# Pooled attention into a gated MLP on one core: transposing the probabilities on VectorE and by DMA instead of on TensorE

## The chip, the cores and the metric

The kernel runs on one core of a Trainium2 chip. The metric is the device time of one execution in microseconds (us); each version is timed in several executions, and the median counts. A profiled execution gives the trace from which all rows below are copied.

## The reference

Attention over pooled keys and values, 8 batches of 8 heads, 576 tokens, head size 64, and after it a multilayer product on all 4608 tokens:

```python
pool = 8                      # Sp = 576 / 8 = 72 pooled keys
k_p = k.reshape(B, H, Sp, pool, D).mean(axis=3)
v_p = v.reshape(B, H, Sp, pool, D).mean(axis=3)
scores = scale * np.matmul(q, k_p.transpose(0, 1, 3, 2))
attn = np.exp(scores - max); attn = attn / (sum + 1e-09)
x = np.matmul(attn, v_p)      # then (4608, 512), heads side by side
a = x @ w1;  b = x @ w2       # 512 -> 1024 each
out = ((a * b) @ w3) @ w_out  # 1024 -> 1024 -> 512
```

All arrays are float32. The kernel multiplies w3 and w_out once at the start, and it splits the operands of its products in a high and a low part of TensorE's 32-bit format (`F32R`), so that one product is three matmuls.

## The kernel before, in words

The 4608 tokens are cut into 12 chunks of 384. Three chunks hold two batches. Chunks 1, 4, 7, 10 contain the end of one batch and the start of the next, so their tokens go in four tiles of 96; the others go in three tiles of 128.

One plan orders everything. `at(kind, k, fn, ...)` puts a function at plan place `k`; the list is sorted by step (the whole part of `k`), within a step by kind (L loads, P work of the vector and scalar engines, M matmuls of the product, A matmuls of the attention), then by the fraction of `k`, then by the order of entry, and the functions are called in that order. Each engine executes its instructions in program order, and each DMA is issued by the SP queue in program order.

MoE chunk m takes 24 steps from M0 + 24 m: for each j of eight, `a_mm` (step 3j), `b_mm` (3j + 1) and `out_mm` of an earlier j (3j + 5), three steps of some 2.1 us on TensorE. Their results lie in PSUM tiles "a" and "b" of one buffer each: `a_post` (ScalarE, 3j + 1) copies a, `b_post` (3j + 2) multiplies it with b on VectorE (L545) and makes its high part on ScalarE (L546), `g_lo` (3j + 2.5) its low part on VectorE (L551). The bank of "b" is free for the next j when L545 is done. `out_post` of the chunk before stores its result at step 3.

Under MoE chunk m the attention of chunk n = m + 1 is prepared. For each tile t: `s_mm` computes the scores in two halves of four heads (TensorE, L404); `soft1` takes the minimum of a half, subtracts, exponentiates and sums (VectorE L420, L422, L426, ScalarE L425); `soft2` divides (L439, L441, L442), with the probabilities in E, a tile of 8 heads x 72 keys; `soft3` puts the 8 keys of each head that do not fit in the 64-key layout into R, high and low parts (L451, L453). Then `pt_mm` and `ptr_mm` transpose E (four 128-column blocks, L464) and R (two, L474) on TensorE into PSUM, and `pt_post` and `ptr_post` take them from there: ScalarE makes the high part PTh (L486) and copies the rest PTr (L491), VectorE subtracts for the low part PTl (L487). `av_mm` multiplies them with the pooled values for one pair of heads (L499 to L502), and `av_post` writes xT, the input of the next MoE chunk.

Beside that, in the same plan: queries are loaded by `load_q` (L265) and turned by VectorE block transposes in `tr_q` (L276); keys are loaded by `load_k` (L307) and summed over eight on GpSimd (`pool_tree`, L362 to L364); values by `load_v` and `load_vr` (L343, L356). For each batch `prep_v2` splits the pooled values on ScalarE (L374) and GpSimd (L375), and `prep_vr` sums the remaining values on GpSimd and then casts them on ScalarE (L381 to L384). For batches 2 to 7 they stand in steps 9, 10 and 10 of MoE chunks 2, 3, 5, 6, 8 and 9.

The places of a chunk's attention come from these lines at the end:

```python
s0, pt, av = (3, 5.5, 20.5) if n == 1 else (0, 6, 17) if nt == 4 else (0, 5, 15)
s_at = [k + s0 + 3 * t for t in range(nt)]
plan_att(n, s_at, 1, [x + pt for x in s_at], [k + av + pr for pr in range(NPR)])
```

In `p1`, every tile name has one buffer; in `p2`, two.

Of the kernel before, what the change touches and what calls it, by code (L numbers as in the profile page):

```python
# [8 lines left out]
F32 = mybir.dt.float32  # L9
F32R = mybir.dt.float32r  # L10
I32 = mybir.dt.int32
AF = mybir.ActivationFunctionType
ALU = mybir.AluOpType
# [5 lines left out]
def kernel(  # L19
# [14 lines left out]
    nc = tc.nc  # L34
# [3 lines left out]
    P = 128  # L38
# [3 lines left out]
    KR = KP - KM  # L42
    MK0 = (KR, 0)
    RK0 = (0, KM)
    NPR = H // 2
# [4 lines left out]
    CH = 384  # L50
# [9 lines left out]
    p1 = ctx.enter_context(tc.tile_pool(name="p1", bufs=1))  # L60
    p2 = ctx.enter_context(tc.tile_pool(name="p2", bufs=2))
# [9 lines left out]
    VR = [cp.tile([P, NPR, P], F32R, name=f"VR{i}") for i in range(2)]  # L71
# [4 lines left out]
        out=msk,  # L76
        in_=ident.rearrange("p (a two e) -> p two a e", two=2, e=2 * KR),
        axis=AX.XY,
        op=ALU.add,
# [8 lines left out]
    def f(ap):  # L88
        return ap.bitcast(F32)
# [11 lines left out]
    def W_cell(s, i, dt):  # L101
        return cp.tile([P, DM], dt, tag=f"W{s}_{i}", name="Wc")
# [48 lines left out]
    def split(src, hi, lo, eng=nc.vector):  # L151
        nc.scalar.copy(out=hi, in_=src)
        eng.tensor_tensor(out=lo, in0=src, in1=f(hi), op=ALU.subtract)  # L153

    def w_tiles(s):
        if s == 0:
            stage["wt"] = [t[:, i] for t, x in (
                (p1.tile([P, x, 512], I32, tag=tag, name="wt"), x)
                for tag, x in (("PTh", 3), ("PTl", 3), ("PTr", 1))) for i in range(x)]
        if s < NJ:  # L160
            stage["wo", s] = stage["wt"][s % 4], f(stage["wt"][4 + s % 3])
        stage["w3", s] = W_cell(0, 4 + s % 4, I32), W_cell(1, 4 + s % 4, F32)

    def w_block(v):
# [3 lines left out]
        if new:  # L168
            w_tiles(v)
            r3, z3 = stage["w3", v]  # L170
            ro, zo = stage["wo", v]
            high(raw["w3", v], z3)
            low(raw.pop(("w3", v)), r3)
            high(raw["wo", v], zo)
# [34 lines left out]
    def w_conv(s):  # L209
        w_tiles(s)  # L210
        conv_a(raw.pop(("w3", s)), *stage["w3", s])
# [28 lines left out]
    def pieces(n):  # L240
        i, r = divmod(n, 3)
        if r == 0:
            return [(2 * i, 0, 384, 0)]
        if r == 1:
            return [(2 * i, 384, 192, 0), (2 * i + 1, 0, 192, 192)]
        return [(2 * i + 1, 192, 384, 0)]

    def tok_tiles(n):
        res = []
        for (b, s0, cnt, off) in pieces(n):  # L250
            step = 128 if cnt == 384 else 96
            for x in range(0, cnt, step):
                res.append((b, off + x, step))
        return res
# [137 lines left out]
            nc.gpsimd.tensor_tensor(  # L392
                out=VR[b % 2][rows, r // 2::2, D * par:D * par + D], in0=hi[rows], in1=m[rows], op=ALU.add)

    Et, Mt, PTh, PTl, PTr, xT = {}, {}, {}, {}, {}, {}

    Sp = {}

# [35 lines left out]
    Rt = {}  # L434
# [10 lines left out]
    def soft3(n, t):  # L445
        b, off, nt = tok_tiles(n)[t]
        E = Et[n, t]
        R = Rt[n, t] = p2.tile([P, NPR, 2, 2, 2, KR], F32R, tag="R", name="R")
        er = E[:nt].rearrange("p (a h) (x e) -> p a (h x) e", h=2, e=KR)[:, :, 0:18:17, :]
        for dup in range(2):  # L450
            nc.scalar.copy(out=R[:nt, :, :, dup, 0], in_=er)  # L451
        for dup in range(2):
            nc.vector.tensor_tensor(  # L453
                out=R[:nt, :, :, dup, 1], in0=er, in1=f(R[:nt, :, :, dup, 0]), op=ALU.subtract)

    Tp = {}
# [11 lines left out]
    def ptr_mm(n, t):  # L468
        b, off, nt = tok_tiles(n)[t]
        R = f(Rt[n, t].rearrange("p a h u s e -> p (a h u s e)"))  # L470
        ps = patt.tile([P, 512], F32, tag="att", name="att")
        rv = ps[:, :2 * P].rearrange("p (a c) -> p a c", c=P)
        for g in range(2):
            nc.tensor.transpose(  # L474
                out=rv[:, g, :nt], in_=R[:nt, g * P:(g + 1) * P], identity=ident[:nt, :nt])
        Tp[n, t, "r"] = rv

    def pt_post(n, t):
        b, off, nt = tok_tiles(n)[t]
        if t == 0:  # L480
            PTh[n] = p1.tile([P, NPR, CH], F32R, tag="PTh", name="PTh")
            PTl[n] = p1.tile([P, NPR, CH], F32R, tag="PTl", name="PTl")
            PTr[n] = p1.tile([P, 2, CH], F32R, tag="PTr", name="PTr")
        pv = Tp.pop((n, t))
        hi, lo = PTh[n][:, :, off:off + nt], PTl[n][:, :, off:off + nt]
        nc.scalar.copy(out=hi, in_=pv[:, :, :nt])  # L486
        nc.vector.tensor_tensor(out=lo, in0=pv[:, :, :nt], in1=f(hi), op=ALU.subtract)  # L487

    def ptr_post(n, t):
        b, off, nt = tok_tiles(n)[t]  # L490
        nc.scalar.copy(out=PTr[n][:, :, off:off + nt], in_=Tp.pop((n, t, "r"))[:, :, :nt])  # L491

    def av_mm(n, pr):
        ps = patt.tile([P, 512], F32, tag="att", name="att")
        for (b, s0, cnt, off) in pieces(n):
            c = slice(off, off + cnt)
            vh, vl = (vbd[b % 2][s][:, pr] for s in range(2))
            o = ps[:, c]
            nc.tensor.matmul(out=o, lhsT=vh, rhs=PTh[n][:, pr, c], start=True, stop=False)  # L499
            nc.tensor.matmul(out=o, lhsT=vh, rhs=PTl[n][:, pr, c], start=False, stop=False)  # L500
            nc.tensor.matmul(out=o, lhsT=vl, rhs=PTh[n][:, pr, c], start=False, stop=False)  # L501
            nc.tensor.matmul(out=o, lhsT=VR[b % 2][:, pr], rhs=PTr[n][:, pr // 2, c], start=False, stop=True)  # L502
        Tp[n, pr, "x"] = ps

    def av_post(n, pr):
# [93 lines left out]
    def at(kind, k, fn, *args):  # L599


        plan.append((k // 1, "LPMA".index(kind), k % 1, len(plan), fn, args))

    def plan_att(n, s_at, ds, pt_at, av_at):


        for t in range(len(tok_tiles(n))):
            for half in range(2):
                k = s_at[t] + ds * half
                at("A", k, s_mm, n, t, half)  # L610
                at("P", k + 1, soft1, n, t, half)
            at("P", k + 2, soft2, n, t)
            at("P", k + 3, soft3, n, t)
            k = pt_at[t]
            at("A", k, pt_mm, n, t)
            at("A", k, ptr_mm, n, t)
            at("P", k + 1, pt_post, n, t)
            at("P", k + 1, ptr_post, n, t)
        for pr in range(NPR):
            at("A", av_at[pr], av_mm, n, pr)  # L620
            at("P", av_at[pr] + 1, av_post, n, pr)
# [17 lines left out]
    def plan_q(n, load, d_load, turn, d_turn):  # L639
        for pr in range(NPR):  # L640
            at("L", load + d_load * pr, load_q, n, (pr,))
            at("P", turn + d_turn * pr, tr_q, n, pr)

    def plan_q3(n, load, turn):
        for pr in range(NPR):
            at("L", load[pr], load_q3, n, pr)
            at("A", turn[pr], q3_turn, n, pr)
            at("P", turn[pr] // 1 + 1.2, q3_post, n, pr)
# [10 lines left out]
    for s in range(NS):  # L659
        k = F0 + 2 * s  # L660
# [3 lines left out]
        else:  # L664
# [9 lines left out]
    plan_q3(0, [K0 - 10.5 + 1.5 * pr for pr in range(NPR)], [K0 - 3, K0 - 2, K0 - 1, K0])  # L674
    plan_v(0, K0 - 4.5, K0 + 5.5, K0 + 2, K0 + 11, K0 + 8.5)
    plan_att(0, [K0 + 3, K0 + 2.5, K0 + 6.5], 0.5, [K0 + 6.5, K0 + 8.5, K0 + 11.5],
             [K0 + 14, K0 + 14.5, K0 + 14.5, K0 + 14.5])


    for j in range(NJ):  # L680
        for w in range(2):
            i = 2 * j + w
            at("L", K0 + 8.5 + i, load_w12, j, w)
            k = M0 - 6 + 1.25 * i
# [5 lines left out]
    for m in range(NCH):  # L690
        m0 = M0 + 3 * NJ * m
        for j in range(NJ):
            k = m0 + 3 * j
# [9 lines left out]
    for n in range(1, NCH):  # L703
        k = M0 + 3 * NJ * (n - 1)
        nt = len(tok_tiles(n))
        s0, pt, av = (3, 5.5, 20.5) if n == 1 else (0, 6, 17) if nt == 4 else (0, 5, 15)
        s_at = [k + s0 + 3 * t for t in range(nt)]
        plan_att(n, s_at, 1, [x + pt for x in s_at], [k + av + pr for pr in range(NPR)])
        if n == 1:
            plan_q3(n, [K0 + 8.5 + 1.5 * pr for pr in range(NPR)], [K0 + 12, K0 + 13, K0 + 15, K0 + 15.5])  # L710
        else:
            plan_q(n, k - 18, 1, k - 9, 1)
    for b in range(1, B):
        k = M0 + 3 * NJ * (3 * (b // 2) + b % 2 - 1)
# [39 lines left out]
```

## Time and profile before

| what | value |
|---|---|
| three executions, median | 807.12 us (804.91 to 807.75) |
| span of the profiled execution, first to last instruction | 803.4 us; its time with what lies around it is not listed apart, the lowest execution is 1.5 us above its span |
| mean granted TensorE clock | 0.989 |
| TensorE busy, matmuls | 777.9 us, 97% |
| VectorE busy | 431.7 us, 54% |
| ScalarE busy | 288.0 us, 36% |
| GpSimd busy | 196.1 us, 24% |
| DMA | 62.63 MB, 30.1% of 16 engines' span |

The page gives the busy share of each engine, the span in 40 slices, the chain of work that ended last, and the costliest groups of instructions. A row of a timeline has the start and the duration in us, the engine, the line and the operation, out<-in with partitions x elements, and in brackets how long the engine sat idle before it and which instruction ended that. A row of the chain has start, duration, engine, tile and line. A row of windows has the stretch, its length, busy time and count of TensorE's matmuls, its weight loads, VectorE, ScalarE and GpSimd, then the granted clock, the DMA share and GB/s. A row of groups has the count, then busy us, the mean ns of one, and the idle time before them. Durations of neighbours on one engine overlap a little; from start to next start is what an instruction takes from its queue.

### The profile page before, as it was taken

To read this page: it belongs to the slowest core of one execution; us is meant where nothing else is said; L and a number is where in the kernel's file an instruction comes from. 1 tells how busy PE (TensorE), PEld (TensorE's weight loads), DVE (VectorE), ACT (ScalarE), POOL (GpSimd) and SP (SyncE) were. 2 spreads that over 40 slices of the span, in tenths; PEclk is the share of its full clock that TensorE was granted. 3 is DMA by queue.
4 is the path that set the end of the run, shared out by engine and by line. 5 is a ranking of instruction groups with operands and counts; after the bars stand their busy time and mean duration, and the time that the engine had idled before them with its cause. 6 is when DMAs were issued, how large, how long until landed. Compare 5 with 4: busy or idle time off the path is not lost.

```text
span 803.4 us, 11625 instructions
## 1 busy us (share of the span) xinstructions
PE 777.9 (97%) x4344; PEld 722.2 (90%) x4344; DVE 431.7 (54%) x873; ACT 288.0 (36%) x727; POOL 196.1 (24%) x234
## 2 busy tenths in 40 slices
PE   7899888999999999999999999999999999999998
PEld 6677777899999999999999999999999999999997
DVE  6968989465373375374374374474454455452112
ACT  5567565332243233242242333232242332332211
POOL 2155465107007302025008102034028020000000
PEclk8999999999999999999999999999999999999999
DMA  9988960045034030062043030071143110100101
GB/s 333 267 206 217 273 145 1 1 94 123 1 72 120 27 80 1 1 143 75 1 95 109 27 67 1 17 157 44 43 85 91 53 26 1 40 1 1 40 1 39
DMA packets 106632, 62.63 MB, mean 78 GB/s; under 512 B 73680, under 2 KB 90320, under 8 KB 106576
## 3 DMA queue, kind: packets, MB, share of 16 engines
q1 hardware_dynamic: 106576, 61.89, 30.1%
q8 instruction: 34, 0.56, 0.3%
q14 instruction: 22, 0.18, 0.1%
HBM read 52.43 MB, written 9.44 MB: 77 GB/s over the span
## 4 chain that ended last, share of the span: by engine, by line
PE 85%; DVE 7%; DMA 4%; issue 2%; ACT 2%; SPq 0%; DVEq 0%
PE o L560 24%; PE a L525 24%; PE b L525 23%; PE att L404 4%; PE o L586 2%; DMA st<-in_k_dram 2%; PE att L464 2%; DVE wb L140 1%; DVE wb L148 1%; PE att L501 1%; PE att L500 1%; PE att L502 1%; PE att L499 1%; PE att L474 1%; DMA raw<-in_moe_w_out_dram 1%
## 5 line engine op out<-in xcount | busy, mean ns | idle before, releaser
L525 PE MATMUL a<-xT,hl 128*128 128x384 f32 x1152 | 223.1, 342 | 0.0
L525 PE MATMUL b<-xT,hl 128*128 128x384 f32 x1152 | 220.3, 339 | 0.4 <-DVE Wc L153 0.4
L525 PEld LDWEIGHTS a<-xT,hl 128*128 128x128 f32 x1152 | 205.0, 190 | 4.9 <-POOL hl L153 0.2
L525 PEld LDWEIGHTS b<-xT,hl 128*128 128x128 f32 x1152 | 198.7, 188 | 0.8 <-DVE Wc L153 0.8
L560 PE MATMUL o<-Wc,gh 128*128 128x512 f32 x576 | 183.6, 400 | 0.0
L560 PEld LDWEIGHTS o<-Wc,gh 128*128 128x128 f32 x576 | 105.1, 189 | 17.3
L545 DVE TENSOR_TENSOR a<-b,a 128x384 f32<-128x384 f32 x96 | 53.1, 553 | 123.5 <-PE b L525 123.5
L362 POOL TENSOR_TENSOR st<-st 72x512 f32<-72x512 f32 (+1 forms) x53 | 73.0, 1377 | 173.2 <-DMA st<-in_k_dram 161.0
L560 PE MATMUL o<-Wc,gl 128*128 128x512 f32 x288 | 114.0, 396 | 0.0
L535 ACT COPY a<-a 128x384 f32<-128x384 f32 x96 | 46.1, 480 | 179.9 <-PE a L525 160.6
L546 ACT CAST gh<-a 128x384 fp32r<-128x384 f32 x96 | 49.2, 512 | 148.4 <-DVE a L545 148.4
L551 DVE TENSOR_TENSOR gl<-a,gh 128x384 fp32r<-128x384 f32 x96 | 59.4, 619 | 35.8 <-ACT gh L546 35.4
L375 POOL TENSOR_TENSOR vbd<-vm,vbd 64x256 fp32r<-64x256 f32 x16 | 13.3, 833 | 249.8 <-ACT vbd L374 248.2
L560 PEld LDWEIGHTS o<-Wc,gl 128*128 128x128 f32 x288 | 54.1, 188 | 12.5
L511 DVE TENSOR_TENSOR xT<-att,xT 128x384 fp32r<-128x384 f32 x48 | 26.5, 556 | 70.0 <-ACT xT L510 70.0
L426 DVE TENSOR_REDUCE sm<-E 128x4 f32<-128x288 f32 (+1 forms) x70 | 31.6, 451 | 46.3 <-ACT E L425 46.3
L404 PE MATMUL att<-kbd,qT 128*128 128x144 f32 (+1 forms) x320 | 52.1, 286 | 0.2 <-ACT E L430 0.2
L420 DVE TENSOR_REDUCE mx<-att 128x4 f32<-128x288 f32 (+1 forms) x80 | 36.0, 450 | 28.8 <-PE att L404 28.7
L425 ACT ACTIVATE E<-E 128x288 f32<-128x288 f32 (+1 forms) x70 | 31.1, 445 | 55.4 <-DVE E L422 55.4
L404 PEld LDWEIGHTS att<-kbd,qT 128*128 128x128 f32 (+1 forms) x320 | 46.6, 179 | 1.1 <-ACT E L430 0.5
L586 PE MATMUL o<-hl 128*128 128x512 f32 x144 | 42.3, 430 | 3.3 <-DVE hl L177 3.3
L363 POOL TENSOR_TENSOR st<-st 72x256 f32<-72x256 f32 (+1 forms) x53 | 41.8, 789 | 4.2
(87 smaller groups left out, 806.4 us busy)
## 6 DMA issues: line engine op xcount, KB each, us to landing
raw<-in_moe_w_dram SPq DMA_DIRECT2D x32, 512.0 KB
st<-in_k_dram SPq DMA_DIRECT2D x32, 288.0 KB
out_dram<-ob SPq DMA_DIRECT2D x35, 256.0 KB
st<-in_v_dram SPq DMA_DIRECT2D x32, 256.0 KB
qs<-in_q_dram SPq DMA_DIRECT2D x128, 48.0 KB
raw<-in_moe_w_out_dram SPq DMA_DIRECT2D x8, 512.0 KB
st<-in_v_dram SPq DMA_DIRECT2D x64, 64.0 KB
qs<-in_q_dram SPq DMA_DIRECT2D x96, 24.0 KB
```

Source lines behind the costliest of these rows:

```text
L362: nc.gpsimd.tensor_tensor(out=t[:, :, 0:4], in0=t[:, :, 0:4], in1=t[:, :, 4:8], op=ALU.add)
L363: nc.gpsimd.tensor_tensor(out=t[:, :, 0:2], in0=t[:, :, 0:2], in1=t[:, :, 2:4], op=ALU.add)
L404: nc.tensor.matmul(out=ps[:nt, 2 * KP * j:2 * KP * (j + 1)], lhsT=qT[n][:, pr, off:off + nt], rhs=kbd[b % 2][:, pr], start=True, stop=True,)
L420: nc.vector.tensor_reduce(out=mx[:nt, hs], in_=sv, axis=AX.X, op=ALU.min)
L426: nc.vector.reduce_sum(out=sm[:nt, hs], in_=E[:nt, hs], axis=AX.X)
L525: nc.tensor.matmul(out=o, lhsT=w12[j, w][sw][:, kt * P:(kt + 1) * P], rhs=x[sx][:, kt], start=(i == 0), stop=(i == 3 * NK - 1))
L535: nc.scalar.copy(out=a, in_=gt[m, j][:, :CH])
L545: nc.vector.tensor_tensor(out=g, in0=ps[:, :CH], in1=g, op=ALU.mult)
L546: nc.scalar.copy(out=gh, in_=g)
L551: nc.vector.tensor_tensor(out=gl, in0=g, in1=f(gh), op=ALU.subtract)
L560: nc.tensor.matmul(out=oacc[m][t], lhsT=(gh, gl)[sg][:, c], rhs=W[j][sw], start=(j == 0 and i == 0), stop=(j == NJ - 1 and i == 2))
L586: nc.tensor.matmul(out=wacc[h][it], lhsT=w3t[s][sa][:, it * P:(it + 1) * P], rhs=wo[j][sb], start=(j == 0 and i == 0), stop=(j == NJ - 1 a ...
```

## The change

For chunks 2 to 11 the TensorE transposes of E and R go, and with them their PSUM tiles. Instead `pt_turn` makes VectorE transpose blocks of 32 x 32, E in one instruction and R in another, into an SBUF tile T of one buffer. A block takes every fourth column (columns 4j + g for one g), so that afterwards T holds on partition j of a 32-token group the columns 4j, 4j + 1, 4j + 2, 4j + 3 next to each other. `pt_move` then issues on SP one SBUF-to-SBUF DMA for each 32 tokens: 32 partitions of four runs of 768 bytes become 128 partitions of one run, in the new tile PTx, which holds for each 32 tokens four slices of E and two of R. `pt_split` makes the high part PTh from PTx on ScalarE and writes the low part over PTx on VectorE. `av_mm` reads PTx in runs of 32 tokens. Chunks 0 and 1 keep the TensorE transposes and write into the new layout. R goes from two buffers to one. The places: scores one step earlier, the turn one step after `soft3`, the moves one step later, the split at 8.5 after the tile's scores (counted from the first half), the value matmuls one step later.

```diff
-                for tag, x in (("PTh", 3), ("PTl", 3), ("PTr", 1))) for i in range(x)]
+                for tag, x in (("PTh", 3), ("PTx", 4))) for i in range(x)]
...
-        R = Rt[n, t] = p2.tile([P, NPR, 2, 2, 2, KR], F32R, tag="R", name="R")
+        R = Rt[n, t] = p1.tile([P, NPR, 2, 2, 2, KR], F32R, tag="T" if (n, t) == (0, 1) else "R", name="R")
...
+    def pt_tiles(n):
+        PTh[n] = p1.tile([P, NPR, CH], F32R, tag="PTh", name="PTh")
+        PTx[n] = p1.tile([P, CH // 32, NPR + 2, 32], F32R, tag="PTx", name="PTx")
+
+    def pt_lo(n, c, w):
+        return PTx[n][:, c.start // 32:c.stop // 32, w].rearrange("p c a i -> p a c i")
+
+    def turn(out, in_):
+        nc.vector.transpose(
+            out=out.rearrange("p g a i -> p a g i"), in_=in_.rearrange("p a (j g) -> p a g j", g=4))
+
+    def pt_turn(n, t):
+        b, off, nt = tok_tiles(n)[t]
+        if t == 0:
+            pt_tiles(n)
+        E = Et[n, t].rearrange("p (a h) k -> p a (h k)", h=2)
+        T = Tp[n, t] = p1.tile([P, 4, NPR + 2, 32], F32, tag="T", name="T")
+        turn(T[:nt, :, :NPR], E[:nt, :, KR:KR + P])
+        turn(T[:nt, :, NPR:], f(Rt[n, t][:nt].rearrange("p (g a) h u s e -> p g (a h u s e)", g=2)))
+
+    def pt_move(n, t):
+        b, off, nt = tok_tiles(n)[t]
+        T = Tp.pop((n, t))
+        for c in range(nt // 32):
+            nc.sync.dma_start(
+                out=f(PTx[n])[:, off // 32 + c].rearrange("p a i -> p (a i)"),
+                in_=T[32 * c:32 * c + 32].rearrange("j g a i -> j g (a i)"))
+
+    def pt_split(n, t):
+        b, off, nt = tok_tiles(n)[t]
+        c = slice(off, off + nt)
+        hi, lo = PTh[n][:, :, c].rearrange("p a (c i) -> p a c i", i=32), pt_lo(n, c, slice(0, NPR))
+        split(f(lo), hi, lo)
...
-            nc.tensor.matmul(out=o, lhsT=vh, rhs=PTl[n][:, pr, c], start=False, stop=False)
+            nc.tensor.matmul(out=o, lhsT=vh, rhs=PTx[n][:, cc, pr], start=False, stop=False)
...
-            nc.tensor.matmul(out=o, lhsT=VR[b % 2][:, pr], rhs=PTr[n][:, pr // 2, c], start=False, stop=True)
+            nc.tensor.matmul(out=o, lhsT=VR[b % 2][:, pr], rhs=PTx[n][:, cc, NPR + pr // 2], start=False, stop=True)
...
+            if n > 1:
+                at("P", k + 4, pt_turn, n, t)
+                at("L", k + 5, pt_move, n, t)
+                at("P", pt_at[t], pt_split, n, t)
+                continue
...
-        s0, pt, av = (3, 5.5, 20.5) if n == 1 else (0, 6, 17) if nt == 4 else (0, 5, 15)
+        s0, pt, av = (3, 5.5, 20.5) if n == 1 else (-1, 8.5, 18) if nt == 4 else (-1, 8.5, 16)
```

More of the change, by code (lines that the diff above doesn't have):

```diff
@@ L393, in prep_vr2 @@
                 out=VR[b % 2][rows, r // 2::2, D * par:D * par + D], in0=hi[rows], in1=m[rows], op=ALU.add)
-    Et, Mt, PTh, PTl, PTr, xT = {}, {}, {}, {}, {}, {}
+    Et, Mt, PTh, PTx, xT = {}, {}, {}, {}, {}
     Sp = {}
@@ L480, in pt_post @@
         if t == 0:
-            PTh[n] = p1.tile([P, NPR, CH], F32R, tag="PTh", name="PTh")
-            PTl[n] = p1.tile([P, NPR, CH], F32R, tag="PTl", name="PTl")
-            PTr[n] = p1.tile([P, 2, CH], F32R, tag="PTr", name="PTr")
+            pt_tiles(n)
         pv = Tp.pop((n, t))
-        hi, lo = PTh[n][:, :, off:off + nt], PTl[n][:, :, off:off + nt]
+        c = slice(off, off + nt)
+        hi, lo = PTh[n][:, :, c], pt_lo(n, c, slice(0, NPR))
         nc.scalar.copy(out=hi, in_=pv[:, :, :nt])
-        nc.vector.tensor_tensor(out=lo, in0=pv[:, :, :nt], in1=f(hi), op=ALU.subtract)
+        nc.vector.tensor_tensor(
+            out=lo, op=ALU.subtract, in0=pv[:, :, :nt].rearrange("p a (c i) -> p a c i", i=32),
+            in1=f(hi).rearrange("p a (c i) -> p a c i", i=32))
     def ptr_post(n, t):
         b, off, nt = tok_tiles(n)[t]
-        nc.scalar.copy(out=PTr[n][:, :, off:off + nt], in_=Tp.pop((n, t, "r"))[:, :, :nt])
+        nc.scalar.copy(
+            out=pt_lo(n, slice(off, off + nt), slice(NPR, NPR + 2)),
+            in_=Tp.pop((n, t, "r"))[:, :, :nt].rearrange("p a (c i) -> p a c i", i=32))
     def av_mm(n, pr):
@@ L495, in av_mm @@
         for (b, s0, cnt, off) in pieces(n):
-            c = slice(off, off + cnt)
+            c, cc = slice(off, off + cnt), slice(off // 32, (off + cnt) // 32)
             vh, vl = (vbd[b % 2][s][:, pr] for s in range(2))
```

## The prediction

> **What bounds the kernel now.** I read the page's first two parts, then the chain that ended last inside two steady chunks, then each engine's timeline there.
>
> ```profile
> PE 777.9 (97%) x4344; PEld 722.2 (90%) x4344; DVE 431.7 (54%) x873; ACT 288.0 (36%) x727; POOL 196.1 (24%) x234
> PEclk8999999999999999999999999999999999999999
> ```
>
> TensorE is busy 97% of the span at nearly full clock. The chain from 268 to 336 us, which holds the steps of MoE chunk 3 while the four 96-token tiles of attention chunk 4 are prepared, is TensorE alone:
>
> ```profile
> 276.95 2.11 PE a L525 x12
> 279.06 0.49 PE att L404 x4
> 279.55 2.08 PE b L525 x12
> 281.64 0.49 PE att L404 x4
> 282.13 2.10 PE o L560 x9
> ...
> 293.58 0.33 PE att L464 x4
> 293.92 0.17 PE att L474 x2
> ```
>
> Each piece starts where the last ended. A plan step is one of a (2.11), b (2.08), o (2.10); scores add 0.49 to some steps, a tile's transposes 0.33 + 0.17 = 0.50. The window of that chunk and the chain in a chunk with three 128-token tiles say the same:
>
> ```profile
> 276.90:336.70 59.80, 59.80 (x354) 56.43 (x353) 31.47 (x73) 19.39 (x51) 6.65 (x9) 1.00 0.12 27
> ```
>
> ```profile
> 409.47 0.44 PE att L464 x4
> 409.91 0.22 PE att L474 x2
> ```
>
> 59.80 busy of 59.80 us at clock 1.00: time taken off TensorE here comes off the end, unless something else becomes late. A 128-token tile's transposes cost 0.66.
>
> **The change, part by part.** *Removed from TensorE.* Chunks 2 to 11 hold 21 tiles of 128 tokens and 12 of 96 (chunks 4, 7, 10): 21 x 0.66 + 12 x 0.50 = 19.9 us. PSUM tiles for them go too; no engine waited for one in the steady part, so that is worth nothing.
>
> *Added to VectorE.* Two block transposes a tile (512 and 256 elements a partition). The same operation exists, on contiguous input; the reduction over pooled keys reads, as the new transposes do, one 4-byte element at a time with a jump of 16 bytes or more (it jumps 256):
>
> ```profile
> 438.18 0.57 DVE L276 STREAM_TRANSPOSE qT<-qs 128x384 f32<-128x384 f32 x1
> 438.67 2.07 DVE L551 TENSOR_TENSOR gl<-a,gh 128x384 fp32r<-128x384 f32 x1
> ```
>
> ```profile
> L319 DVE TENSOR_REDUCE km<-st 72x128 f32<-72x1024 f32 x3 | 5.8, 1933 | 0.3 <-DMA st<-in_k_dram 0.3
> ```
>
> From the first, 384 elements take 0.49 until the next instruction: some 1.04 ns an element and 0.09 fixed, so a pair of 768 elements takes 0.98. From the second, 1933 ns less about 0.1 for 1024 elements is 1.8 ns each, and the pair takes 1.48. These are the ends. I take the middle, 1.23: the operation is that of the first row, the access that of the second, whose price also holds 128 short runs. The Trainium skill (SBUF — State Buffer, "Door 1: The DMA port swizzle", the note on cachelines) says that SBUF has 16-byte lines and that every access that crosses to a new one pays; by that rule, which speaks against this change, the pair takes the 1.48, and the sum would end 2.2 us later than by 1.23. The L319 row agrees in direction; nothing here shows 16 bytes.
>
> *Moved.* The split now comes at plan place 8.5 after a tile's scores, so for tile 1 in step 10.5 (before: step 9 or 10), scores one step earlier, the value matmuls one later. ScalarE loses one PSUM copy a tile (no gain, it is 36% busy). The probability tiles live in SBUF, so the split's two instructions read SBUF; I keep their durations.
>
> The order is what costs. VectorE in a four-tile chunk:
>
> ```profile
> 302.75 0.35 DVE L453 TENSOR_TENSOR R<-E,R 96x64 fp32r<-96x64 f32 x2
> 303.02 0.45 DVE L420 TENSOR_REDUCE mx<-att 96x4 f32<-96x288 f32 x1
> 303.50 0.45 DVE L422 TENSOR_TENSOR E<-att,mx 96x288 f32<-96x288 f32 x1
> 304.47 0.45 DVE L426 TENSOR_REDUCE sm<-E 96x4 f32<-96x288 f32 x1 [0.51 <-ACT E L425]
> 304.84 0.54 DVE L545 TENSOR_TENSOR a<-b,a 128x384 f32<-128x384 f32 x1
> 305.30 0.44 DVE L420 TENSOR_REDUCE mx<-att 96x4 f32<-96x288 f32 x1
> ```
>
> ```profile
> 411.17 0.16 DVE L439 TENSOR_SCALAR sm<-sm 128x8 f32<-128x8 f32 x1
> ...
> 411.61 0.76 DVE L442 TENSOR_TENSOR E<-E,sm 128x576 f32<-128x576 f32 x1
> ```
>
> From start to next start: half a softmax 1.82 (303.02 to 304.84), the remainder's subtractions 0.27, the product L545 0.46 (g_lo taken alike), soft2 about 1.14. A tile then costs VectorE 2 x 1.82 + 1.14 + 0.27 + 1.23 (turn) + 0.92 + 0.48 (split) = 7.7 us, against three steps of 6.3 and two scores, 7.26, on TensorE. So from the first turn on VectorE works without a pause. Counting from the chunk's first a: turn 0 at 9.7 to 10.95, turn 1 to 18.15, turn 2 to 25.96, the second softmax half of tile 3 behind it. Its exponential and what follows on ScalarE, as they stand now:
>
> ```profile
> 303.99 0.44 ACT L425 ACTIVATE E<-E 96x288 f32<-96x288 f32 x1 [1.24 <-DVE E L422]
> 304.46 0.40 ACT L374 CAST vbd<-vm 64x256 fp32r<-64x256 f32 x1
> 308.44 0.30 ACT L381 CAST vrh<-vrm 128x128 fp32r<-128x128 f32 x1 [3.58 <-POOL vrm L364]
> ...
> 309.38 0.50 ACT L546 CAST gh<-a 128x384 fp32r<-128x384 f32 x1
> ```
>
> ```profile
> ACT vrh L381 <- POOL vrm L364: 21.4, 6, 3.6
> ```
>
> ScalarE waits 3.58 us for GpSimd's pooled values, once in each of chunks 2, 3, 5, 6, 8, 9. Today nothing urgent is behind it: L545 has been issued on VectorE before. After the change tile 1's split (10.5) stands behind this wait on ScalarE, its subtraction heads VectorE's queue, and the product L545 of j = 3 (step 11) stands behind that. L545 frees the only bank "b", which b of j = 4 (step 13) needs. Four tiles: exponential at 25.96 + 0.97 = 26.93, L374 27.40, L381 3.98 later 31.38, split 0.94 later 32.32, subtraction 32.83, L545 33.31 to 33.87. TensorE reaches b of j = 4 at 13 x 2.093 + 7 x 0.49 = 30.64. It waits 3.2 us (2.45 with the short turn, 3.95 with the long). Three tiles: L374 follows a's copy at 23.8, L545 ends at 30.5, b is due at 13 x 2.093 + 5 x 0.49 = 29.66: 0.8. Over three chunks of each kind 12.0 us.
>
> *The clock.* Waiting TensorE has its own price:
>
> ```profile
> 133.70 0.44 PE L474 MATMUL att<-ident,R 96*128 96x96 f32 x2 [1.97 <-DVE E L422]
> 143.97 0.36 PE L474 MATMUL att<-ident,R 96*128 96x96 f32 x2 [1.73 <-DVE R L453]
> ```
>
> ```profile
> 132.00:134.00 2.00, 0.30 (x3) 0.33 (x4) 1.52 (x5) 0.41 (x2) 0.48 (x1) 0.96 0.00 0
> 134.00:136.00 2.00, 2.00 (x8) 2.00 (x8) 1.90 (x5) 1.30 (x5) 0.90 (x2) 0.50 0.04 8
> 136.00:138.00 2.00, 2.00 (x10) 2.00 (x9) 1.49 (x4) 1.66 (x5) 1.36 (x3) 0.69 0.00 0
> ...
> 144.00:146.00 2.00, 2.00 (x13) 2.00 (x14) 1.90 (x5) 1.16 (x3) 0.12 (x1) 1.00 0.00 0
> ```
>
> After a pause of 1.97 us the granted clock is half for some 3.4 us (losses 0.08 + 1.00 + 0.62 = 1.7 us); after 1.73 it stays 1.00. So the three pauses of 3.2 cost 1.7 each more: 5.1 us. The 0.8s cost none.
>
> *The moves on SP's queue.* Four copies a tile (three of 96 tokens), in order with everything SP issues:
>
> ```profile
> 402.10 1.91 SPq L575 DMA_DIRECT2D out_dram<-ob  x3
> 404.05 11.89 SPq L265 DMA_DIRECT2D qs<-in_q_dram  x24
> ```
>
> ```profile
> 528.41 0.38 SPq L307 DMA_DIRECT2D st<-in_k_dram  x1
> ```
>
> ```profile
> 532.81 1.28 POOL L362 TENSOR_TENSOR st<-st 72x512 f32<-72x512 f32 x1 [44.56 <-DMA st<-in_k_dram]
> ```
>
> A query load takes SP 11.89 / 24 = 0.50, a key load 0.38, a store up to 0.64; GpSimd starts on a key load 4.0 us after its issue ended. I take 0.38 for a move (as few long runs as a key load) and 3 us to land (a third of the bytes). Move 0 waits for turn 0 and holds query loads, key loads and the next values behind it; these have over ten steps. In MoE chunks 2, 5, 8 the next queries come in two pieces, eight loads for a head pair. There: move 0 to 12.5, eight and eight loads to 20.4, move 1 to 21.9 (landed 24.9, turn 2 needs its tile from about 23 and waits under the 0.8 above), then 16 query and 2 key loads, 8.7 us, to 30.6, move 2 to 32.1, landed 35.1. The split of tile 2, its subtraction and L545 of j = 4 take 1.8: bank "b" free at 36.9, wanted at 16 x 2.093 + 2.45 + 0.8 = 36.7. Cost 0.2 x 3 = 0.5. If a move costs nothing to issue and lands at once, nothing; at 0.64 and 4.0 us the bank is free at 41, and 4.3 + 1.7 us are lost, 18 in all. Elsewhere the loads between moves are half as many and move 2 lands by 30.
>
> *Edits with one answer.* R has one buffer instead of two, and T one. A tile's R is rewritten three steps after the turn that frees it starts (in chunks 0 and 1 after the transposes that still read it), and T is rewritten at the next turn, after its moves have landed; I cost both at nothing. Without that cover a wait is at most what is left of a turn, 1.23, or of a move. The weight staging in the merged tile moves no instruction.
>
> *TensorE's new operands.* Two of four value matmuls stream runs of 32 elements. Nothing before shows it; I take nothing (bounds 0 and, at double the 0.18 of each of the eight in a chunk, 1.4 a chunk).
>
> Sum against this execution: 803.4 - 19.9 + 12.0 + 5.1 + 0.5 = 801.1 us of span. The runs' median, 807.1, stands 3.7 above this span, which I carry over: 804.8 us.
>
> **Rivals.** *Cover holds.* If ScalarE's wait doesn't reach bank "b", or the pauses stay under the 1.7 that leaves the clock alone, the time is between 787.2 (all of 19.9) and 795. For it: L545's old slack of 4 us in step 11 to 13. Against: the programs' order on both engines is fixed, and the 3.58 us is in all six chunks.
>
> *SP is late, slower.* Place: move 2 in chunks 2, 5, 8 behind 34 loads. Every us of landing after 34.9 is a us of TensorE, after 36.9 with the half clock besides; from 2.3 us more a chunk the kernel is slower than before. At the bounds above 822. For it: 0.50 a query load; against: move 0 and 1 have slack.
>
> *Only the clock differs.* The Trainium skill (TensorE: Matmul & The Clock Gate, "What's actually happening") lets the clock fall after an idle window of about 3.4 us that runs free of the program. As a mechanism of this kernel: pauses of 3.2 us leave the clock at 1.00, and the time is 804.8 - 5.1 = 799.7. Against: the pause of 1.97 us above already halved it; the trace disagrees with a whole idle window.
>
> **How the numbers follow.** Half a per cent, 4 us, is about what a measurement of this kernel can tell from no change. Forecast 0.52 (own range 800 to 809 from the turn's ends and 0 to 3 us of SP; a third of it under 803.1); cover holds 0.20; SP late 0.15 (a third of it ending under 811); clock only 0.07; slow operand streams 0.06. Faster 0.17 + 0.19 + 0.04 = 0.40, slower 0.10 + 0.06 + 0.02 = 0.18, the rest 0.42. The range 789 to 812 leaves out most of "SP late" and the full 19.9.
>
> **What would show it.** Right: no L464 and L474 after 160 us; 33 pairs of transposes of 1.0 to 1.5 us; waits of TensorE for VectorE's L545 at L525 (b) some 31 us into chunks 3, 6, 9, 2.4 to 4 us long, with clock 0.5 behind, and shorter ones in 2, 5, 8; three-tile chunks 1, 4, 7, 10 at 56.3 us. Wrong: chunks 3, 6, 9 at 57.8; ScalarE waiting for PTx transfers for long; b or o longer than 2.1; turns outside 0.98 to 1.48.

## The result, and the profile after

The changed kernel takes 824.9 us (median of four, 824.4 to 831.3) beside 806.0 (803.9 to 807.8) of the kernel before: the ratio is 1.0243, with a 95% interval of 1.0201 to 1.0285. I had forecast 804.8 and a range of 789 to 812. It is slower, by more than the range allows.

The first part of the page of the kernel after:

```profile
PE 769.5 (94%) x4146; PEld 712.4 (87%) x4146; DVE 470.3 (57%) x939; ACT 280.1 (34%) x694; POOL 196.6 (24%) x234
```

TensorE has 198 matmuls less and is busy 94% instead of 97% of a longer span (822.6 us instead of 803.4). What it waits for between 150 and 790 us is one thing, by the view of waits (line waited for: us in total, times, longest):

```profile
PE b L563 <- DVE a L583: 26.1, 9, 4.1
```

L583 is the product, L545 in the kernel before; L563 is L525. Of the nine waits, from TensorE's timeline, those of chunks 2, 2, 3 and 6 (5 and 8 are like 2: 1.12 and 3.42, 1.13 and 3.94 us; 9 is like 3: 3.76):

```profile
246.41 2.35 PE L563 MATMUL b<-xT,hl 128*128 128x384 f32 x12 [1.14 <-DVE a L583]
256.69 3.76 PE L563 MATMUL b<-xT,hl 128*128 128x384 f32 x12 [3.73 <-DVE a L583]
313.21 3.27 PE L563 MATMUL b<-xT,hl 128*128 128x384 f32 x12 [3.77 <-DVE a L583]
...
496.22 4.21 PE L563 MATMUL b<-xT,hl 128*128 128x384 f32 x12 [4.05 <-DVE a L583]
```

Three long waits were forecast, in chunks 3, 6 and 9, and three short ones in 2, 5 and 8. They are there. Three more long ones, the second in each of chunks 2, 5 and 8, are what the forecast did not have. After each long wait the twelve matmuls of b take 3.06 to 4.21 us instead of 2.35: the windows behind the waits of chunks 2 and 3 (the granted clock stands third from the end) have about half the clock.

```profile
256.00:258.00 2.00, 1.31 (x4) 1.31 (x5) 1.42 (x4) 0.89 (x2) 0.83 (x2) 0.59 1.07 145
258.00:260.00 2.00, 2.00 (x9) 2.00 (x8) 0.72 (x2) 0.00 (x0) 1.84 (x3) 0.55 1.03 196
...
314.00:316.00 2.00, 2.00 (x10) 2.00 (x9) 2.00 (x5) 1.18 (x4) 1.04 (x1) 0.60 0.00 0
316.00:318.00 2.00, 2.00 (x7) 1.67 (x6) 1.71 (x4) 0.26 (x1) 0.00 (x0) 0.55 0.00 0
```

The length of a chunk is read from SP's timeline, from one chunk's first store to the next one's. Before, the stores that end chunks 0 to 3:

```profile
167.59 1.92 SPq L575 DMA_DIRECT2D out_dram<-ob  x3
225.84 1.91 SPq L575 DMA_DIRECT2D out_dram<-ob  x3
284.08 1.91 SPq L575 DMA_DIRECT2D out_dram<-ob  x3
343.86 1.91 SPq L575 DMA_DIRECT2D out_dram<-ob  x3
```

And after:

```profile
165.58 1.51 SPq L613 DMA_DIRECT2D out_dram<-ob  x2
221.91 1.98 SPq L613 DMA_DIRECT2D out_dram<-ob  x3
285.07 1.97 SPq L613 DMA_DIRECT2D out_dram<-ob  x3
348.51 1.98 SPq L613 DMA_DIRECT2D out_dram<-ob  x3
```

Chunk 1 went from 58.25 to 56.33 us, the gain in full; chunk 2 from 58.24 to 63.16; chunk 3 from 59.78 to 63.44. The next groups of three are much alike: 56.32, 62.98 and 64.82, then 56.32, 63.55 and 64.50.

### The profile page after: what moved, and what is told of

Same layout as the page of the kernel before. It is cut to its first block, busy times and chain, and to the rows that moved or that the text cites. A ratio compares the mean times of both kernels' runs of the same rounds, so it can differ in the third digit from the quotient of the medians.

```text
span 822.6 us, 11446 instructions
## 1 busy us (share of the span) xinstructions
PE 769.5 (94%) x4146; PEld 712.4 (87%) x4146; DVE 470.3 (57%) x939; ACT 280.1 (34%) x694; POOL 196.6 (24%) x234
## 4 chain that ended last, share of the span: by engine, by line
PE 64%; DVE 15%; DMA 8%; SPq 4%; ACT 4%; issue 3%; POOL 2%; DVEq 0%; ACTq 0%; POOLq 0%
PE b L563 20%; PE o L598 18%; PE a L563 17%; DVE T L487 2%; PE att L404 2%; SPq L265 2%; DMA st<-in_k_dram 2%; SPq L503 2%; DMA PTx<-T 2%; DMA qs<-in_q_dram 2%; DVE mx L420 1%; DVE E L422 1%; ACT E L425 1%; DMA raw<-in_moe_w_dram 1%; DVE E L442 1%
## 5 line engine op out<-in xcount | busy, mean ns | idle before, releaser
L563 PE MATMUL b<-xT,hl 128*128 128x384 f32 x1152 | 229.7, 349 | 26.6 <-DVE a L583 26.1
L563 PEld LDWEIGHTS b<-xT,hl 128*128 128x128 f32 x1152 | 206.1, 194 | 29.8 <-DVE a L583 28.9
L563 PE MATMUL a<-xT,hl 128*128 128x384 f32 x1152 | 223.4, 342 | 0.0
L563 PEld LDWEIGHTS a<-xT,hl 128*128 128x128 f32 x1152 | 203.9, 190 | 4.5 <-POOL hl L153 0.2
L598 PEld LDWEIGHTS o<-Wc,gh 128*128 128x128 f32 x576 | 108.9, 192 | 17.5
L583 DVE TENSOR_TENSOR a<-b,a 128x384 f32<-128x384 f32 x96 | 53.0, 552 | 103.2 <-PE b L563 103.2
L584 ACT CAST gh<-a 128x384 fp32r<-128x384 f32 x96 | 49.3, 513 | 160.0 <-DVE a L583 160.0
L573 ACT COPY a<-a 128x384 f32<-128x384 f32 x96 | 45.9, 479 | 114.6 <-PE a L563 92.4
L153 DVE TENSOR_TENSOR PTx<-PTx,PTh 128x512 fp32r<-128x512 f32 (+1 forms) x33 | 22.2, 673 | 72.0 <-ACT PTh L152 71.6
```

The costliest lines, as they stand in the source:

```text
L563: nc.tensor.matmul(out=o, lhsT=w12[j, w][sw][:, kt * P:(kt + 1) * P], rhs=x[sx][:, kt], start=(i == 0), stop=(i == 3 * NK - 1))
L573: nc.scalar.copy(out=a, in_=gt[m, j][:, :CH])
L583: nc.vector.tensor_tensor(out=g, in0=ps[:, :CH], in1=g, op=ALU.mult)
L584: nc.scalar.copy(out=gh, in_=g)
L598: nc.tensor.matmul(out=oacc[m][t], lhsT=(gh, gl)[sg][:, c], rhs=W[j][sw], start=(j == 0 and i == 0), stop=(j == NJ - 1 and i == 2))
```

## The experiments

Two theories were set against each other first. The order theory says that the split stands ahead of the product on VectorE and so hands every lateness of what it needs (pooled values, turned tiles) to bank "b". The transfer theory says that the moves on SP are late whatever stands behind them. A third, that VectorE has too much work, was kept as a rival.

**The split behind the product.** One number of the plan for each kind of chunk:

```diff
-(-1, 8.5, 18) if nt == 4 else (-1, 8.5, 16)
+(-1, 9.75, 18) if nt == 4 else (-1, 9.75, 16)
```

> The split at 9.75 instead of 8.5 after a tile's scores: for tile 1 in step 11.75 and for tile 2 in 14.75, behind the product of b (steps 11 and 14) and its low part on VectorE's queue. Order theory (TensorE waits only because the product that frees bank b is queued behind a split that waits): all nine waits of TensorE for the product go, about 26 us of waiting and 8 us of half clock, and the time falls from 824.9 to 787 to 791 us. Transfer theory (the moves on SP are late, and someone waits for them wherever the split stands): the 3.4 to 3.9 us waits of chunks 2, 5, 8 stay in some form, 805 us or more. VectorE theory (it is overfull, with 1.53 us for a turn): the 3.8 to 4.1 us waits of chunks 3, 6, 9 stay, 803 us or more.

Measured: 802.8 us, ratio 0.9947 [0.9928, 0.9965]. That is 22 us better than the change, and none of the theories' figures. No wait for the product is left: all nine reached bank "b" by the order. But in chunks 2, 5 and 8 the late tile now meets its own user, the value matmuls (L537, L538), and in chunks 3, 6 and 9 the next user of ScalarE, L584, is late. From TensorE's timeline:

```profile
260.66 0.44 PE L537 MATMUL att<-PTh,vbd 128*128 128x384 f32 x1 [1.79 <-ACT PTh L152]
261.57 0.69 PE L538 MATMUL att<-PTx,vbd 128*128 128x384 f32 x1 [0.47 <-DVE PTx L153]
315.08 0.74 PE L598 MATMUL o<-Wc,gh 128*128 128x512 f32 x2 [1.00 <-ACT gh L584]
```

So both theories hold a part: the order takes the lateness to bank "b", and the transfer is late by itself.

**The query loads behind the moves.** Only the places of the next queries' loads and turns change, for chunks 3 and later:

```diff
-            plan_q(n, k - 18, 1, k - 9, 1)
+            plan_q(n, *((k - 18, 1, k - 9, 1) if n == 2 else (k - 12.5, 1, k - 5, 1)))
```

> The query loads of chunks 3 to 11 go behind the last moves on SP's queue (steps 11.5 to 14.5 instead of 6 to 9), their block transposes on VectorE four steps later; the split stays at 8.5. Order and transfer theories alike: move 2 of chunks 2, 5, 8 is issued some 13 us earlier, the waits of 3.4 to 3.9 us with the half clock behind them go, 16 us in all: 808 to 810 us; the waits of about 1.1 us in the same chunks and 3.8 to 4.1 us in chunks 3, 6, 9 stay. If SP's queue is not what delays move 2, no change: 824 us.

Measured: 811.5 us, 1.0061 [1.0038, 1.0085], 1.5 over what I expected. The second wait of chunks 2, 5 and 8 is gone; the first ones (1.13, 1.14, 1.13) and those of chunks 3, 6 and 9 (3.77, 4.05, 3.77) stay. SP's queue made the former and not the latter.

**The pooled values behind the product.** The last argument of one `plan_v` call, k + 10, becomes k + 11.75, so that GpSimd's sum and ScalarE's casts of the remaining values come later.

> The pooled remaining values are prepared at step 11.75 instead of 10 in MoE chunks 2, 3, 5, 6, 8, 9, so that ScalarE's wait for GpSimd stands behind the split of tile 1 and the product of b. Order theory: the waits of chunks 3, 6, 9 go with their half clock, 15 to 17 us; in chunks 2, 5, 8 the first wait of 1.1 goes and the second grows by as much, since the last move is not earlier: 808 to 810 us. VectorE theory: chunks 3, 6, 9 keep most of their wait, 818 us or more.

Measured: 813.0 us, 1.0078 [1.0051, 1.0105], 3 over what the order theory expected. The waits in chunks 3, 6 and 9 went, but a new one came in 2, 5 and 8. GpSimd's and ScalarE's timelines in chunk 2:

```profile
254.60 1.29 POOL L362 TENSOR_TENSOR st<-st 72x512 f32<-72x512 f32 x1 [6.95 <-DMA st<-in_k_dram]
```

```profile
259.80 0.30 ACT L381 CAST vrh<-vrm 128x128 fp32r<-128x128 f32 x1 [7.97 <-POOL vrm L364]
...
260.73 0.46 ACT L573 COPY a<-a 128x384 f32<-128x384 f32 x1
```

The sum moved behind the key sum of the same step, which waits for a key load that is late on SP; the casts waited for the sum, and a's copy L573 stood behind the casts. TensorE then waited 5.01, 5.23 and 5.75 us for bank "a". The edit moved a stall to another queue.

**Both, split and values.** The two edits above together.

> Both: the split at 9.75 and the remaining values at 11.75. Order theory: no wait of TensorE for the product, 787 to 788 us, at most 3 us below the split's move alone, since there ScalarE's wait for GpSimd still delays the high part of the product, about 1 us in each of chunks 3, 6, 9. Transfer theory: 805 us or more. VectorE theory: 803 us or more.

Measured: 813.8 us, 1.0078 [1.0061, 1.0096]; far from what I expected, by the same new wait for L573 (17.3 us in three). It taught what to move: the casts alone.

**The casts late.** GpSimd's sum stays at its place; only ScalarE's three casts of the remaining values move behind the product's place, from 10 to 11.75.

```diff
         pool_tree(stage.pop(("vr", b)), m)
-        nc.scalar.copy(out=hi, in_=m)
+        stage["vrt", b] = hi, m
...
+        late = 1.75 if b > 1 else 0
+        at("P", prep_r + late, cast_vr, b)
+        at("P", prep_r + 1 + late, prep_vr2, b)
```

> Only ScalarE's casts of the remaining values go from step 10 to 11.75, their sums on GpSimd stay in step 10, ahead of the next key sums. The split stays at 8.5. Order theory: in chunks 3, 6, 9 the wait of 3.8 to 4.1 us before b of j = 4 and the half clock behind it go, some 15 us; in chunks 2, 5, 8 the 1.1 us wait goes and the wait for move 2 grows by as much: 808 to 811 us. VectorE theory: with 1.53 us a turn it reaches the product late in any case; at least 1.5 us of each wait in chunks 3, 6, 9 stays: 815 us or more.

Measured: 810.1 us, 1.0044 [1.0023, 1.0064], as expected. Nothing is waited for in chunks 3, 6 and 9; 0.17 of the first waits of 2, 5 and 8 is left, in one of the three; the second ones remain, 4.88, 4.32 and 5.17. So ScalarE's wait for GpSimd, with the split behind it, made six of the nine waits, and SP's queue the other three.

**All repairs.** Split at 9.75, queries behind the moves, casts late.

> Split at 9.75, query loads behind the moves, casts of the remaining values at 11.75 with their sums left in step 10. Order theory with the transfer's own wait removed too: TensorE waits for nothing in chunks 2 to 11, three-tile chunks 56.3 us and four-tile chunks 57.8 us long, 786 to 790 us. If the moves or VectorE hold TensorE wherever they are put: 797 us or more.

Measured: 788.3 us (786.7 to 792.4), 0.9776 [0.9730, 0.9823]: faster than both kernels, by 1.8 to 2.7% than the kernel before. TensorE waits for nothing between 150 and 790 us. Its busy shares, and its stores:

```profile
PE 759.8 (96%) x4146; PEld 703.9 (89%) x4146; DVE 481.9 (61%) x939; ACT 279.4 (35%) x694; POOL 200.2 (25%) x234
```

```profile
170.31 1.99 SPq L617 DMA_DIRECT2D out_dram<-ob  x3
226.63 1.98 SPq L617 DMA_DIRECT2D out_dram<-ob  x3
282.97 1.97 SPq L617 DMA_DIRECT2D out_dram<-ob  x3
340.91 2.06 SPq L617 DMA_DIRECT2D out_dram<-ob  x3
...
682.09 2.34 SPq L617 DMA_DIRECT2D out_dram<-ob  x3
```

Chunk 2 takes 56.34 us and chunk 3 57.94. VectorE does all the turns here, too, and is busier than in the slow kernel, so its amount of work alone was not the cause; the next run shows that it sets a part of the size.

**The turn without the stride.** The block transposes read neighbouring columns instead of every fourth; the columns come out in another order, so the output is another.

```diff
-in_=in_.rearrange("p a (j g) -> p a g j", g=4)
+in_=in_.rearrange("p a (g j) -> p a g j", g=4)
```

> The changed kernel, but the turn takes neighbouring columns for a block instead of every fourth, so its input has no stride; the columns come out in another order and the result is another. If the stride makes the turn dear: a pair of transposes takes 0.98 us instead of 1.53, the waits of chunks 3, 6, 9 shrink by three turns' difference, 1.65 us each, the others by up to 0.55: 817 to 820 us. If the price is the instruction's own: 1.5 us a pair, and 824 to 825 us.

Measured: 817.8 us, 1.0136 [1.0085, 1.0188], inside what I expected. The groups of VectorE (ns: least, median, most) in this kernel:

```profile
L487 DVE STREAM_TRANSPOSE T<-E x33: 697/701/714, 173.5 to 726.0; 128x512 f32<-128x512 f32 x21, 96x512 f32<-96x512 f32 x12
L487 DVE STREAM_TRANSPOSE T<-R x33: 394/402/403, 174.1 to 726.6; 128x256 f32<-128x256 f32 x21, 96x256 f32<-96x256 f32 x12
```

And in the kernel after:

```profile
L487 DVE STREAM_TRANSPOSE T<-E x33: 1079/1092/1119, 168.9 to 734.2; 128x512 f32<-128x512 f32 x21, 96x512 f32<-96x512 f32 x12
L487 DVE STREAM_TRANSPOSE T<-R x33: 576/589/640, 169.9 to 735.3; 128x256 f32<-128x256 f32 x21, 96x256 f32<-96x256 f32 x12
```

By the medians the pair is 0.58 us shorter. In chunk 3 the wait fell from 3.77 to 2.06, by 1.71, or three turns' worth (6 and 9 alike: by 1.72 and 1.70): there VectorE does pace the lateness, as the prediction counted it.

**A fifth copy.** To every 128-token tile one more copy on SP, of 16 KB (128 runs of 128 bytes) into a tile that nothing reads.

```diff
+        if nt == P:
+            z = p1.tile([P, 32], F32, tag="Z", name="Z")
+            nc.sync.dma_start(out=z, in_=T[:32, :, 0])
```

> The changed kernel with a fifth copy for each 128-token tile, 128 runs of 128 bytes from the same T into a scratch tile nobody reads. Issue theory (a move costs SP 0.6 us whatever its bytes, and move 2 of chunks 2, 5, 8 stands behind all of them): two or three more issues ahead of the last landing, 1.2 to 1.9 us more waiting in each of those three chunks, 829 to 832 us. If the bytes or the landing set the wait: within 1 us of the changed kernel, 824 to 826 us.

Measured: 831.2 us, 1.0294 [1.0268, 1.0321], the time as expected. SP's timeline:

```profile
240.84 2.50 SPq L503 DMA_DIRECT2D PTx<-T  x4
243.39 0.60 SPq L508 DMA_DIRECT2D Z<-T  x1
```

The extra copy has a sixth of a move's bytes and takes SP as long as a move, 0.60 us. The second waits of chunks 2, 5 and 8 grew from 3.73, 3.42 and 3.94 to 4.71, 4.55 and 4.71: by 0.8 to 1.1, less than the 1.2 to 1.9 I expected, for two more issues of 0.60 ahead of the last move. By their bytes two such copies would add a sixth of two moves, 0.2 us; so the queue's issue time sets these waits, not the bytes.

**The kernel before, its split moved behind the values.** No turns and no moves: in the kernel before, `pt_post` and `ptr_post` come half a step later in four-tile chunks and one and a half steps later in three-tile ones, behind ScalarE's wait for GpSimd.

> The kernel before, with TensorE's transposes; only pt_post and ptr_post of chunks 2 to 11 go later by half a step (four tiles) or one and a half (three), so that tile 1's stands behind ScalarE's wait for the remaining values and ahead of the product of b, as in the changed kernel. Order theory: the same wait appears without any VectorE transpose or move, 0.7 us in each of chunks 2, 5, 8 and 1.3 us in 3, 6, 9, short enough to leave the clock alone: 4 to 8 us over the kernel before. Transfer and VectorE theories: no change.

Measured: 818.8 us, 1.0153 [1.0121, 1.0185]; more than expected, and at another place:

```profile
253.63 0.44 PE L474 MATMUL att<-ident,R 128*128 128x128 f32 x2 [2.00 <-ACT PTr L491]
```

TensorE waited for the PSUM tiles that the late posts free, 2.00 us in chunks 2, 5 and 8 and 0.40 in 3, 6 and 9, and not for bank "b". It shows that a split in this place costs a kernel without any turn, too; on bank "b" it says nothing. The waits are 7.2 us. The other 5 us are longer matmuls: between the first and the tenth store TensorE is busy 534.1 us with 3014 matmuls, 528.8 in the kernel before with as many. More than half of that is in chunks 5 and 8 (60.0 us busy each, 58.5 in chunk 2), where the granted clock fell to 0.50 after the pause; after the same pause in chunk 2 it stayed at 1.00.

**Chunk 1 turned as well.** All repairs, with chunk 1's tiles turned on VectorE (split at 8.75 there).

> All three repairs, and chunk 1 (prepared under MoE chunk 0, which converts w1 and w2 at the same time) uses the VectorE turn and the moves too, its split at 8.75. If TensorE's 9 us of waits there come from transposes standing ahead of the product in its order: they go with 2 us of transposes and up to 3 us of half clock, 776 to 784 us. If VectorE, 8 to 9 tenths busy there, sets the pace: 786 to 792 us.

Measured: 788.4 us, 0.9761 [0.9734, 0.9787], the same as without. In the four stretches of 10 us from 110 to 150 us VectorE is busy 10.00, 9.49, 9.39 and 9.38 us, and TensorE waits as long as without (9.6 us beside 9.9 from 100 to 172 us), now chiefly for VectorE's product, 5.08 us at the longest. That fits VectorE setting the pace under chunk 0, so that less work for TensorE buys nothing there; no run has taken work off VectorE in this stretch.

## Why the prediction was wrong

**Removed from TensorE: right.** Between the stores that end chunks 0 and 9 the repaired kernel needs 682.09 - 170.31 = 511.8 us and the kernel before 528.8 (its tenth store begins at 696.37): 17.0 less in nine chunks, where 17.9 was counted. Three-tile chunks came to 56.3 as forecast.

**The order: right in place, a little short in size.** VectorE without a long pause up to the exponential of the last tile, the split behind ScalarE's wait, the product behind the split: chunk 3 on ScalarE and then on VectorE,

```profile
310.67 0.30 ACT L381 CAST vrh<-vrm 128x128 fp32r<-128x128 f32 x1 [3.54 <-POOL vrm L364]
...
311.60 0.49 ACT L152 CAST PTh<-PTx 128x384 fp32r<-128x384 f32 x1
```

```profile
312.13 0.56 DVE L153 TENSOR_TENSOR PTx<-PTx,PTh 128x384 fp32r<-128x384 f32 x1 [4.95 <-ACT PTh L152]
312.60 0.55 DVE L583 TENSOR_TENSOR a<-b,a 128x384 f32<-128x384 f32 x1
```

It came to 3.77, 4.05 and 3.76 us where I had 3.2, and to 1.14, 1.12 and 1.13 where I had 0.8: 15.0 together against 12.0. The turn explains it:

```profile
225.25 1.09 DVE L487 STREAM_TRANSPOSE T<-E 128x512 f32<-128x512 f32 x1
226.27 0.59 DVE L487 STREAM_TRANSPOSE T<-R 128x256 f32<-128x256 f32 x1
226.78 0.41 DVE L420 TENSOR_REDUCE mx<-att 128x4 f32<-128x288 f32 x1
```

From start to next start it takes 1.53 us, beyond the long end of 1.48, and not the 1.23 I took; by the long end I had 3.95. The long end itself counts the fixed 0.1 us once for two instructions; counted twice, as in the short end, it is 1.58, and the turn lies inside. The middle was the wrong choice between a row with the right operation and one with the right access: the access decided.

**The moves on SP's queue: the step that failed.** "I take 0.38 for a move (as few long runs as a key load)" made this term 0.5 us; it came to 11.1 us of waiting. SP's queue in chunk 2, whose first a starts at 215.3:

```profile
226.92 2.57 SPq L503 DMA_DIRECT2D PTx<-T  x4
229.53 7.86 SPq L265 DMA_DIRECT2D qs<-in_q_dram  x16
237.50 2.51 SPq L503 DMA_DIRECT2D PTx<-T  x4
240.06 4.00 SPq L265 DMA_DIRECT2D qs<-in_q_dram  x8
244.16 0.36 SPq L307 DMA_DIRECT2D st<-in_k_dram  x1
244.56 5.17 SPq L265 DMA_DIRECT2D qs<-in_q_dram  x8
249.83 0.36 SPq L307 DMA_DIRECT2D st<-in_k_dram  x1
250.28 2.50 SPq L503 DMA_DIRECT2D PTx<-T  x4
```

The order of issues is the one worked out, 34 loads with the moves among them. A set of four moves takes the queue 2.56 us instead of 1.52, so twelve cost 3.1 more; the loads between the second and third set took 1.5 more than the 8.7 I had (one of them alone took 1.86). The first set began 0.7 later than the 10.95 I had. The landing was faster than my 3 us, which gave 1 back. By the 3.1 alone bank "b" would have been free at 40.0 us where it was wanted at 36.7: the price of an issue is enough for a long wait. The chain that ended last shows the end of it:

```profile
252.18 2.55 DMA PTx<-T
...
254.83 0.63 ACT PTh L152
...
256.17 0.48 DVE a L583
...
256.69 3.76 PE b L563 x12
```

The last move landed at 254.7, 39.4 us into the chunk and not 35.1, and bank "b" was free at 41.3 us, where my upper bounds (0.64 to issue, 4.0 to land) had put it. That they met is in part luck: the landing took 2 us, not 4, and the later start and the slow load made up for it. The 0.64 is a third of the row of three stores, between which SP waits; one store takes 0.37.

So the rival "SP is late" came true, at its place, on top of the forecast's waits. It waits 11.1 us in three chunks, and three more spells of half clock follow.

The rows do not bear out a price by the number of runs, from which I took the 0.38. By the kernel, a key load has 144 runs and a store 128, at some 0.37; a move has 128, at 0.60; and a load of the remaining values has 32, at 0.62. That last price stood in the kernel before, on SP's queue in chunk 2 (eight issues, with the gaps between them):

```profile
260.24 5.40 SPq L356 DMA_DIRECT2D st<-in_v_dram  x8
```

**The clock: right in kind, short in number and size.** Six long waits instead of three. Between the first and the tenth store the kernel after takes 551.4 us (the tenth begins at 717.00), 39.6 more than the repaired one; 26.1 of it are waits, and the remaining 13.5, or 2.25 a long wait, where I had 1.7, is TensorE taking longer for the same 2833 matmuls (busy 525.4 us, 511.8 in the repaired kernel), with half the clock behind the long waits.

The sum, with measured terms, between those stores: 528.8 - 17.0 + 26.1 + 13.5 = 551.4 (13.5 is what the others leave); start-up and end took 3.4 less than in the execution before, and the span is 822.6 instead of 803.4. Of the 21.5 us by which my span was short, the moves with their half clock are 11.1 + 6.75 - 0.5 = 17.3, the long waits of chunks 3, 6 and 9 with theirs 3.6, the short ones 1.0, and the rest, part of it the start-up, nearly cancels.

**The rest.** T's single buffer made four waits of VectorE for a move, 9.5 us in all. With the query loads behind the moves they are gone and the first waits of chunks 2, 5 and 8 stay at 1.13, so TensorE did not feel them. The value matmuls took 0.17 to 0.18 us each as before (0.17, 0.18, 0.18, 0.18 in chunk 2's chain): the operand streams cost nothing.

## What to carry to other kernels

Work taken off the bounding engine pays only if what replaces it doesn't stand, in any in-order queue, between that engine's results and their consumer: write down each queue's order around the new instructions, and put those that wait for other engines or for DMAs behind those that free a PSUM bank. A DMA that is newly on the path to a deadline must not stand behind loads that have time; price its issue by the dearest copy that the trace shows until one of the same shape has been timed (here copies cost from 0.37 to 0.62 us, and neither the bytes nor the number of runs gave the order), and if the answer changes sign inside the bounds, put more chance on the bad end. All three repairs here are places in a plan, and they turn 2.4% slower into 2.2% faster.

## What the runs showed of the hardware

- A copy from SBUF to SBUF with 128 runs takes SP's queue 0.60 us to issue with runs of 768 bytes and of 128 bytes alike; a move of 96 KB landed some 2 us after its issue ended (2.55 after it began).
- A block transpose that reads one 4-byte element every 16 bytes takes 1092 and 589 ns for 512 and 256 elements a partition, 701 and 402 ns with neighbours. That is 1.96 ns an element against 1.17, from the differences. The Trainium skill (SBUF — State Buffer, "Door 1: The DMA port swizzle", the note on cachelines) says that an access that crosses to a new 16-byte line pays. These runs agree in direction; with one stride alone they do not show that the border lies at 16 bytes.
- Pauses of 1.1 us left the clock at 1.00; pauses of 3.4 us and more halved it each time. Between them it went both ways: in the kernel before with its split moved, pauses of 2.00 us left it at 1.00 in chunk 2 and halved it in chunks 5 and 8. In the kernel whose turn has no stride, a pause of 2.06 us was followed by slow matmuls (clock 0.54 to 0.61) and one of 2.61 by fast ones (1.00). The Trainium skill (TensorE: Matmul & The Clock Gate, "What's actually happening") has a free-running window of about 3.4 us that must be idle. That it runs free agrees with pauses that go both ways; that the whole of it must be idle doesn't agree with 2.00 and 2.06. From the timeline of TensorE in the kernel whose turn has no stride:

```profile
315.32 3.31 PE L563 MATMUL b<-xT,hl 128*128 128x384 f32 x12 [2.06 <-DVE a L583]
...
440.46 2.38 PE L563 MATMUL b<-xT,hl 128*128 128x384 f32 x12 [2.61 <-DVE a L583]
```
